# Second layer pair of a gated MLP: three groups of 1024 tokens and two of 768 instead of six of 768

## The chip, the cores and the metric

The program runs on one core of one Trainium2 chip. The metric is the device time of one execution in microseconds, the median of several runs. The profile is of one execution.

## What is computed

A linear-attention layer feeds two feed-forward layers; all inputs and the output are float32. The reference, cut to what matters:

```python
kv = einsum('bhsd,bhse->bhde', k, v)            # 8 batches, 8 heads, 576 tokens, 64 wide
out = einsum('bhsd,bhde->bhse', q, kv)
x = out / sqrt(mean(out * out, -1) + 1e-6) * g_norm     # -> 4608 tokens x 512
x = (sigmoid(x @ w_gate) * (x @ w_val)) @ w_out         # 512 -> 1536 -> 512
h = x @ w_in                                            # 512 -> 2048
g = where(h >= 1, h, where(h <= -1, 0, (h + 1)**2 / 4))
return g @ w_out2                                       # 2048 -> 512
```

## The kernel before

All matrix products run on TensorE with float32 split into two fp32r halves: a product of two tiles is three matmuls (high by high, high by low, low by high). Everything in the program is in an order written out by hand; each engine, and SP's one DMA queue, works through its own instructions in that order, and a wait at the head holds what is behind it.

The first half of the time is attention and the first feed-forward layer, on blocks of 512 tokens. The second layer is the class `Second`, which takes its input from DRAM (`x2d`), where the first layer has stored it.

`Second` works on groups of tokens. A group of 768 tokens is two halves of 384 (T2). For each of eight steps s, two blocks of 128 hidden units for both halves of the tokens are formed by a Strassen-like scheme: seven products instead of eight (`product`, L787), each of two blocks by three matmuls = six matmuls, 128x384. The weights for it (`w_load`, seven sums of blocks, 1792 KB a step) and the sums of input blocks (`x_steps`, tiles x_b11, x_t1 and so on) are made beforehand. The products of a step go to four PSUM banks, A to D, in this order: a11 to A, a12 to D, s1 to B, s2 on top of A, a22 to C, s4 on top of B, s3 on top of A. Between them, ScalarE copies partial sums out (`saved`, tiles p1, p5, u2, u3 in the buffers "sv") and VectorE adds them. The last two readers of A in a step are the copy u3 on ScalarE and VectorE's add into g1, which waits for u3's place in the order. The first bank alternates from step to step: `spare((g + s) % 2)` gives bank A or a bank of the accumulators' pool, "acc2_3".

The activation needs, for each block, a clip and a maximum on VectorE and a square on ScalarE; `finish` (L943) does it for two blocks at once, 768 columns. The results are split into halves (`high` on ScalarE, `low` on VectorE, buffers "gsp", four of them) and are the stationary side of the output products (`out_product`, L813): for each 128 tokens three matmuls 128x512. Two of the four results of a step (first half of the tokens) go into the group's accumulators `acc` while the next step's chain runs: one output product (nine matmuls for three blocks of 128 tokens) stands between s1 and s2 and one behind s3, from step 1 on. The results for the second half of the tokens stay in SBUF (g1) and are multiplied after the eight steps, sixteen output products into `acc2` (banks B, C and the spare one), with the eviction of `acc` (`put`) and the x steps of the next group between them. Only the last group ends its last three output products token by token.

Around the first group: `second.begin()` (L1360) issues `x_load(0)` while the first layer's last pair of blocks still runs. In the last loop of output products there (f = 1 to 11, `down`, twelve matmuls each), each round splits the next g (tiles gh, gl), then runs one x step, then issues weight loads (`stream`, tiles woh), and w_load(0) at f = 4, w_load(1) at f = 9. `second.rest()` then opens the other pools and runs the groups.

In `group`, the order around a step's end is:

```python
self.product(A, "s3", "t3", False)
u3 = self.saved(A, "u3")
tt(g1[s][:, 1], A[:, :T2], s5, ALU.add)
tt(c0[:, 1], C[:, :T2], u3, ALU.add)
if late is not None:
    self.out_product(acc, s - 1 + HF, late_hi, False, False)
```

In step 0 `late` is None and no output product stands there.

Of the kernel before, what the change touches and what calls it, by code (L numbers as in the profile page):

```python
# [17 lines left out]
T2 = 384  # L18
# [15 lines left out]
def attn_gated_mlp_kernel(ctx: ExitStack, tc: tile.TileContext, a: dict, out: bass.AP):  # L34
# [669 lines left out]
    class Second:  # L704
        OPS = ("a11", "a12", "a22", "s1", "s2", "s4", "s3")

        def __init__(self):
            self.stack = ExitStack()
            self.xop = self.pool("xop", 1)
            self.st = self.pool("st", 2)  # L710
            self.tmp = self.pool("tmp2", 1)
            self.half = self.tmp.tile([P, 1], F32, name="half2")
            nc.gpsimd.memset(self.half, 0.5)
            self.ws, self.xo = {}, {}
# [10 lines left out]
        def one(self, name, tag, bufs):  # L725
            return self.tmp.tile([P, T2], F32, name=name, tag=tag, bufs=bufs)

# [3 lines left out]
        def spare(self, n):  # L731

            if n == 0:
                return self.bank("A")
            return self.acc_p.tile([P, T], F32, name="acc2_3", tag="acc2_3")


        def w_load(self, s):
            t = self.st.tile([P, 7, 2, 2 * P], F32R, name="wst", tag="st")
            nc.sync.dma_start(out=t.bitcast(F32), in_=w2d[s])  # L740
            return {name: (t[:, i, 0], t[:, i, 1]) for i, name in enumerate(self.OPS)}


        def x_load(self, g):
            t = self.st.tile([P, 7, 2, 2 * P], F32, name="xin", tag="st")
            t = t.rearrange("p a b n -> p (a b n)")[:, 0:8 * T2].rearrange("p (c n) -> p c n", c=KC)
            step = 2 * P
            for k in range(2):
                for i in range(2 * T2 // step):
                    j, off = divmod(g * 2 * T2 + i * step, T)  # L750
                    c = slice(2 * k, 2 * k + 2)
                    nc.sync.dma_start(out=t[:, c, i * step:(i + 1) * step], in_=x2d[j][:, c, off:off + step])
            return t

        def x_split(self, name, src):
            o = self.xop.tile([P, 2, 2, T2], F32R, name=f"x_{name}", tag=name)
# [4 lines left out]
        def x_steps(self, x):  # L761

            b11, b12, b21, b22 = (x[:, 2 * k:2 * k + 2, e * T2:(e + 1) * T2] for k in range(2) for e in range(2))
            self.x_split("b11", b11)
            yield
            t1 = self.pair("t1")
# [5 lines left out]
            t2 = self.pair("t2")  # L772
# [3 lines left out]
            t4 = self.pair("t4")  # L776
# [5 lines left out]
            t3 = self.pair("t3")  # L782
# [4 lines left out]
        def product(self, bank, w, x, first=True):  # L787
            for c in range(2):
                sl = slice(c * P, (c + 1) * P)
                for n, (h, l) in enumerate(((0, 0), (0, 1), (1, 0))):  # L790
                    nc.tensor.matmul(bank[:, :T2], self.ws[w][h][:, sl], self.xo[x][:, l, c], start=first and c == n == 0,  # L791
                                     stop=c == 1 and n == 2, skip_group_check=True)

        def saved(self, bank, name):
            t = self.one(name, "sv", 4)
            act_copy(t, bank[:, :T2])
# [8 lines left out]
        def high(self, src):  # L805
            o = self.gsp.tile([P, 2, T2], F32R, name="gh2", tag="gsp")
# [6 lines left out]
        def out_product(self, acc, f, g, first, last):  # L813
            w = self.wo2[f]
            for t in range(T2 // P):
                mm3(acc[t], (g[:, 0], g[:, 1]), (w[:, 0], w[:, 1]), first, last, slice(t * P, (t + 1) * P))

        def put(self, acc, t0):
            for t in range(T2 // P):
                e = self.pair("ev2").rearrange("p a b -> p (a b)")[:, :T]  # L820
                (act_copy if t % 2 else dve_copy)(e, acc[t])
                nc.sync.dma_start(out=out[t0 + t * P:t0 + (t + 1) * P, :], in_=e)
# [8 lines left out]
        def rest(self):  # L831
            self.ch_p = self.pool("chain", 1, space=bass.MemoryType.PSUM)
            self.wo2p = self.pool("wo2", 1, "left")
            self.gst = self.pool("gst", 1, "left")
            self.gsp = self.pool("gsp", 4, "left")
            self.acc_p = self.pool("acc2", 1, "left", space=bass.MemoryType.PSUM)
            self.wo2 = {}
            groups = NT // (2 * T2)
            for g in range(groups):
                self.group(g, g + 1 < groups)  # L840
            self.stack.close()

        def group(self, g, more):
            tt, g1 = self.tt, {}
            acc = [self.acc_p.tile([P, T], F32, name=f"acc2_{t}", tag=f"acc2_{t}") for t in range(3)]
            late = None
            for s in range(HF):
                A = self.spare((g + s) % 2)
                D, B, C = (self.bank(n) for n in "DBC")
# [9 lines left out]
                c0 = self.tmp.tile([P, 2, T2], F32, name="c0", tag="c0", bufs=2)  # L859
                g1[s] = self.gst.tile([P, 2, T2], F32, name=f"g1_{s}", tag=f"g1_{s}")  # L860
                self.product(A, "a11", "b11")
                s1 = self.saved(A, "p1")
                if late is not None:
                    vl = self.one("v", "v", 2)
# [4 lines left out]
                tt(c0[:, 0], D[:, :T2], s1, ALU.add)  # L869
# [4 lines left out]
                v = self.one("v", "v", 2)  # L874
# [16 lines left out]
                tt(g1[s][:, 0], B[:, :T2], u2, ALU.add)  # L891
                self.product(A, "s3", "t3", False)
                u3 = self.saved(A, "u3")
                tt(g1[s][:, 1], A[:, :T2], s5, ALU.add)
                tt(c0[:, 1], C[:, :T2], u3, ALU.add)
# [7 lines left out]
            vl = self.one("v", "v", 2)  # L903
# [10 lines left out]
            acc2 = [self.bank("B"), self.bank("C"), self.spare(g % 2)]  # L914
# [3 lines left out]
            kept = []  # L918
# [16 lines left out]
            for t in range(T2 // P if kept else 0):  # L935
                for f, h in kept:
# [505 lines left out]
```

## Time and profile before

| | |
|---|---|
| median of 3 runs | 1711.57 us (1710.27 to 1712.14) |
| the profiled execution | 1714.51 us, its span 1712.7 us |
| TensorE busy | 1699.3 us, 8516 matmuls |
| VectorE, ScalarE busy | 1085.9 us, 815.9 us |
| DMA | 343.45 MB, mean 201 GB/s |
| granted TensorE clock, mean | 0.993 of full speed |
| second layer, first chain product | 961.53 us after the span's start |

Matmuls are pipelined and their ends are modelled, so the time that one takes is read from the distance of two starts, not from its length in a row. Engines are PE (TensorE; PEld its weight loads), DVE (VectorE), ACT (ScalarE), POOL, and SPq (SyncE's DMA queue). L791 is line 791 of the kernel before. In a tile's name the buffer number is left out: chA is a chain bank, acc an accumulator's pool.

### The profile page before, as it was taken

Reading aid. Unit: us, or ns where it says so; the run is one execution under the profiler, and the core shown is the slowest. Engines: PE = TensorE matmul, PEld = TensorE weight load, DVE = VectorE, ACT = ScalarE, POOL = GpSimd, SP = SyncE. Lnnn points to the kernel's source line nnn. Section 1 sums busy time; section 2 is a strip of 40 time slices with the busy share of each in tenths; the row PEclk is TensorE's granted clock in tenths of the full one; section 3 lists DMA queues with packets and bytes.
Section 4 is the critical chain, followed back from the end, with each engine's and each line's share of the span. In section 5 each row is a group of like instructions: output and inputs, shape, how many; then the busy total and the mean of one; then the engine's idle time right before and its main releaser. Section 6 shows DMA issues by size and latency. Waiting matters only on the chain.

```text
span 1712.7 us, 23020 instructions
## 1 busy us (share of the span) xinstructions
PE 1699.3 (99%) x8516; PEld 1437.7 (84%) x8516; DVE 1085.9 (63%) x1909; ACT 815.9 (48%) x1388; POOL 1.0 (0%) x8
## 2 busy tenths in 40 slices
PE   8999999999999999999999999999999999999999
PEld 6778878887877877778887898998998998998997
DVE  5888856767746767775666556556556556556553
ACT  3444444635558667744444444444344344444442
POOL 0000000000000000000000000000000000000000
PEclk8999999999999999999999999999999999999999
DMA  9577877668663987678886764442442542442431
GB/s 263 177 256 239 262 244 234 212 212 266 208 200 122 300 298 239 234 253 307 281 300 211 278 241 150 148 172 99 160 160 99 190 144 90 185 166 104 163 116 37
DMA packets 156832, 343.45 MB, mean 201 GB/s; under 512 B 15400, under 2 KB 64680, under 8 KB 150576
## 3 DMA queue, kind: packets, MB, share of 16 engines
q1 hardware_dynamic: 156720, 341.98, 58.9%
q8 instruction: 67, 1.10, 0.3%
q14 instruction: 45, 0.37, 0.1%
HBM read 264.85 MB, written 77.07 MB: 200 GB/s over the span
## 4 chain that ended last, share of the span: by engine, by line
PE 94%; DMA 2%; DVE 2%; ACT 1%; issue 0%; SPq 0%; ACTq 0%; DVEq 0%
PE acc L96 10%; PE acc L94 10%; PE acc L95 10%; PE h L94 6%; PE chB L791 6%; PE h L96 6%; PE h L95 6%; PE pA L647 6%; PE chA L791 4%; PE acc L791 4%; PE pE L647 4%; PE chC L791 3%; PE chD L791 3%; PE pC L647 2%; PE pD L647 2%; PE chC L96 1%
## 5 line engine op out<-in xcount | busy, mean ns | idle before, releaser
L94 PE MATMUL acc<-gh,woh 128*128 128x512 f32 x420 | 165.7, 395 | 2.1 <-DMA woh<-wo1d 2.1
L95 PE MATMUL acc<-gl,woh 128*128 128x512 f32 x420 | 164.4, 391 | 0.3 <-DVE gl L77 0.3
L94 PE MATMUL h<-xh,w 128*128 128x512 f32 x384 | 151.8, 395 | 1.2 <-DVE xn L302 1.2
L96 PE MATMUL h<-xh,w 128*128 128x512 f32 x384 | 150.0, 391 | 0.0
L95 PE MATMUL h<-xl,w 128*128 128x512 f32 x384 | 149.8, 390 | 0.0
L96 PE MATMUL acc<-wo,gh 128*128 128x512 f32 x336 | 132.4, 394 | 0.0
L95 PE MATMUL acc<-wo,gh 128*128 128x512 f32 x336 | 132.2, 394 | 0.0
L94 PE MATMUL acc<-wo,gh 128*128 128x512 f32 x336 | 130.9, 390 | 0.0
L96 PE MATMUL acc<-gh,woh 128*128 128x512 f32 x324 | 126.6, 391 | 0.0
L647 PE MATMUL pA<-xc,wc 128*128 128x512 f32 x432 | 110.2, 390 | 0.5 <-ACT s L69 0.5
L69 ACT ACTIVATE gh<-g 128x384 fp32r<-128x384 f32 (+1 forms) x120 | 63.6, 541 | 73.5 <-PE acc L96 51.7
L94 PEld LDWEIGHTS acc<-gh,woh 128*128 128x128 f32 x420 | 78.9, 188 | 22.3 <-ACT gh L69 3.2
L647 PEld LDWEIGHTS pA<-xc,wc 128*128 128x128 f32 x432 | 80.9, 188 | 18.1 <-ACT s L69 1.2
L95 PEld LDWEIGHTS acc<-gl,woh 128*128 128x128 f32 x420 | 78.9, 188 | 17.8 <-DVE gl L77 1.3
L94 PEld LDWEIGHTS h<-xh,w 128*128 128x128 f32 x384 | 72.2, 188 | 23.2 <-issue 5.9
L720 DVE TENSOR_TENSOR gh<-c,gh 128x384 fp32r<-128x384 f32 x96 | 53.6, 558 | 57.6 <-ACT gh L69 56.9
L720 DVE TENSOR_TENSOR c<-chD,p 128x384 f32<-128x384 f32 x48 | 26.8, 558 | 92.1 <-ACT v L803 81.4
L96 PEld LDWEIGHTS h<-xh,w 128*128 128x128 f32 x384 | 72.2, 188 | 15.2
L95 PEld LDWEIGHTS h<-xl,w 128*128 128x128 f32 x384 | 72.2, 188 | 14.3
L569 DVE TENSOR_TENSOR gf<-sig,h 128x512 f32<-128x512 f32 x57 | 39.1, 686 | 71.1 <-PE h L96 40.4
L720 DVE TENSOR_TENSOR g<-vp,g 128x768 f32<-128x768 f32 x48 | 46.0, 959 | 48.3 <-ACT vp L803 48.3
L96 PEld LDWEIGHTS acc<-wo,gh 128*128 128x128 f32 x336 | 63.0, 188 | 13.6
(236 smaller groups left out, 3828.7 us busy)
## 6 DMA issues: line engine op xcount, KB each, us to landing
wst<-w2d SPq DMA_DIRECT2D x48, 1792.0 KB, 7.4
wc<-w1d SPq DMA_DIRECT2D x168, 256.0 KB, 5.3
woh<-wo1d SPq DMA_DIRECT2D x162, 256.0 KB, 5.0
raw<-in_w SPq DMA_DIRECT2D x32, 512.0 KB, 6.0
raw<-in_w_gv SPq DMA_DIRECT2D x24, 512.0 KB, 5.1
w1d<-w2half SPq DMA_DIRECT2D x48, 256.0 KB, 3.3
w2d<-w2half SPq DMA_DIRECT2D x48, 256.0 KB, 3.9
kvraw<-in_kv_main SPq DMA_DIRECT2D x24, 448.0 KB, 5.6
```

Of the source, the lines that this page charges most:

```text
L69: nc.scalar.activation(out=o, in_=i, func=AF.Copy)
L94: nc.tensor.matmul(ps, w[0][:, wsl], x[0], start=first, stop=False)
L95: nc.tensor.matmul(ps, w[0][:, wsl], x[1], start=False, stop=False)
L96: nc.tensor.matmul(ps, w[1][:, wsl], x[0], start=False, stop=last)
L569: nc.vector.tensor_tensor(out=g, in0=sig, in1=value, op=ALU.mult)
L647: nc.tensor.matmul(o, w[:, h, sl], x[c][l], start=first and c == n == 0, stop=c == 1 and n == 2, skip_group_check=True)
L720: nc.vector.tensor_tensor(out=o, in0=x, in1=y, op=op)
L791: nc.tensor.matmul(bank[:, :T2], self.ws[w][h][:, sl], self.xo[x][:, l, c], start=first and c == n == 0, stop=c == 1 and n == 2, skip_grou ...
```

## The change

Groups are of 2 x 512, 2 x 512, 2 x 512, 2 x 384 and 2 x 384 tokens. A wide group has four blocks of 128 tokens in each half and so four accumulators; the banks are now A, D, B, C for the chain and acc2_0 to acc2_3, and the first product of every step uses A. All tiles have room for 512 columns and are cut to the group's width. To fit, there are two "pair" buffers instead of three, three "sv" and three "gsp" instead of four; `finish` takes its two blocks one after the other through the "v" buffers, and `put` uses "sv" and "v" buffers. `put` handles one block of 128 tokens; for `acc` it is called after output products 1 to 4, one block each. The last three output products of every group are done token block by token block, each block's eviction right behind. `x_load` moves pieces of up to 512 columns instead of 256. The scratch pool and its constant are opened in `rest`, on the other side of SBUF.

```diff
-T2 = 384
+SIZES = (512, 512, 512, 384, 384)
 ...
-    def pair(self, name):
-        return self.tmp.tile([P, 2, T2], F32, name=name, tag="pair", bufs=3)
+    def pair(self, name, n):
+        return self.sums.tile([P, 2, T], F32, name=name, tag="pair")[:, :, :n]
 ...
     def x_load(self, g):
-        step = 2 * P
+        n = 2 * SIZES[g]
+        t = self.st.tile([P, KC, 2 * T], F32, name="xin", tag="st")[:, :, :n]
+        begin = 2 * sum(SIZES[:g])
         for k in range(2):
+            c, at = slice(2 * k, 2 * k + 2), 0
+            while at < n:
+                j, off = divmod(begin + at, T)
+                step = min(T - off, n - at)
+                nc.sync.dma_start(out=t[:, c, at:at + step], in_=x2d[j][:, c, off:off + step])
+                at += step
 ...
-    def put(self, acc, t0):
-        for t in range(T2 // P):
-            e = self.pair("ev2").rearrange("p a b -> p (a b)")[:, :T]
+    def put(self, acc, t0, t):
+        e = self.one("ev2", *(("sv", 3), ("v", 2))[t == 3], T)
 ...
     def group(self, g, more):
-        acc = [self.acc_p.tile([P, T], F32, name=f"acc2_{t}", tag=f"acc2_{t}") for t in range(3)]
+        n2 = self.n = SIZES[g]
+        tokens = range(n2 // P)
+        acc = [self.acc_p.tile([P, T], F32, name=f"acc2_{t}", tag=f"acc2_{t}") for t in tokens]
         for s in range(HF):
-            A = self.spare((g + s) % 2)
-            D, B, C = (self.bank(n) for n in "DBC")
+            A, D, B, C = (self.bank(n) for n in "ADBC")
 ...
-        acc2 = [self.bank("B"), self.bank("C"), self.spare(g % 2)]
+        acc2 = [self.bank(n) for n in "ADBC"[-len(tokens):]]
         for n, f in enumerate(order):
-            if not more and n >= F2 - 3:
-                kept.append((f, ready.pop(n)))
-            else:
-                self.out_product(acc2, f, ready.pop(n), n == 0, n == F2 - 1)
+            if n < F2 - 3:
+                self.out_product(acc2, f, ready.pop(n), n == 0, False)
             if n == 1:
                 self.finish(g1[HF - 1])
                 self.out_product(acc, F2 - 1, late_hi, False, True)
-                self.put(acc, g * 2 * T2)
+            if 0 < n <= len(tokens):
+                self.put(acc, t0, n - 1)
 ...
-        self.put(acc2, g * 2 * T2 + T2)
+        for t in tokens:
+            for n in range(F2 - 3, F2):
+                self.out_product(acc2, order[n], ready[n], False, n == F2 - 1, (t,))
+            self.put(acc2, t0 + n2, t)
 
     def finish(self, c):
-        v = self.pair("vp")
-        self.clip(v, c)
-        self.square(v)
-        self.tt(c, v, c, ALU.max)
+        for e in range(2):
+            v = self.one("v", "v", 2, self.n)
+            self.clip(v, c[:, e])
+            self.square(v)
+            self.tt(c[:, e], v, c[:, e], ALU.max)
```

## Rows read from the trace of the kernel before

**Rows 1.** The page: busy time of each engine, then the chain's shares.

```profile
PE 1699.3 (99%) x8516; PEld 1437.7 (84%) x8516; DVE 1085.9 (63%) x1909; ACT 815.9 (48%) x1388; POOL 1.0 (0%) x8
...
PE 94%; DMA 2%; DVE 2%; ACT 1%; issue 0%; SPq 0%; ACTq 0%; DVEq 0%
```

**Rows 2.** Windows, first group: stretch, length, busy time by engine, clock, DMA, GB/s.

```profile
961.53:1086.07 124.54, 124.54 (x625) 112.70 (x624) 70.24 (x127) 53.56 (x98) 0.00 (x0) 1.00 0.57 213
```

**Rows 3.** Timeline, TensorE in one step: start, length, engine, line, operation, idle before.

```profile
1244.02 0.39 PE L94 MATMUL acc<-wo,gh 128*128 128x512 f32 x1
...
1246.10 1.23 PE L791 MATMUL acc<-x_t,wst 128*128 128x384 f32 x6
1247.17 1.20 PE L791 MATMUL chC<-x_t,wst 128*128 128x384 f32 x6
1248.21 1.20 PE L791 MATMUL chB<-x_b,wst 128*128 128x384 f32 x6
```

**Rows 4.** Timeline, TensorE in the first layer's pair loop, one step apart.

```profile
728.33 1.52 PE L647 MATMUL pC<-xc,wc 128*128 128x512 f32 x6
...
740.57 1.52 PE L647 MATMUL pC<-xc,wc 128*128 128x512 f32 x6
```

**Rows 5.** Timeline and page: around step ends, A's readers, finish; an add at 512.

```profile
1217.88 1.20 PE L791 MATMUL acc<-x_b,wst 128*128 128x384 f32 x6
...
1218.08 0.49 ACT L69 ACTIVATE u<-chA 128x384 f32<-128x384 f32 x1 [1.63 <-PE chA L791]
1218.61 0.56 DVE L720 TENSOR_TENSOR g<-chA,p 128x384 f32<-128x384 f32 x1 [0.94 <-ACT u L69]
...
1247.35 0.55 DVE L800 TENSOR_SCALAR vp<-g 128x768 f32<-128x768 f32 x1
...
1247.93 0.94 ACT L803 ACTIVATE vp<-vp,half 128x768 f32<-128x768 f32 x1
...
1251.08 0.56 DVE L720 TENSOR_TENSOR g<-acc,p 128x384 f32<-128x384 f32 x1 [0.75 <-ACT u L69]
...
1252.38 1.23 PE L791 MATMUL chA<-x_b,wst 128*128 128x384 f32 x6
...
L569 DVE TENSOR_TENSOR gf<-sig,h 128x512 f32<-128x512 f32 x57 | 39.1, 686 | 71.1 <-PE h L96 40.4
```

**Rows 6.** Timeline, first layer: a product that waits for the copy of its bank.

```profile
585.34 0.58 ACT L69 ACTIVATE s<-pA 128x512 f32<-128x512 f32 x1
...
585.98 1.66 PE L647 MATMUL pA<-xc,wc 128*128 128x512 f32 x6 [0.53 <-ACT s L69]
```

**Rows 7.** Timeline, the last output products of the first layer: splits and x steps.

```profile
949.31 0.68 DVE L77 TENSOR_TENSOR gl<-g,gh 128x512 fp32r<-128x512 f32 x1
...
950.89 0.85 ACT L69 ACTIVATE x_t<-t 128x768 fp32r<-128x768 f32 x1 [1.97 <-DVE t L720]
...
951.77 0.96 DVE L720 TENSOR_TENSOR x_t<-t,x_t 128x768 fp32r<-128x768 f32 x1 [0.91 <-ACT x_t L69]
...
952.65 0.68 DVE L77 TENSOR_TENSOR gl<-g,gh 128x512 fp32r<-128x512 f32 x1
...
953.42 0.47 PE L95 MATMUL acc<-gl,wok 128*128 128x512 f32 x1
```

**Rows 8.** Timeline: SP's issue of weight loads, and TensorE's wait for them.

```profile
931.53 7.35 SPq L540 DMA_DIRECT2D woh<-wo1d  x12
...
936.61 0.47 PE L94 MATMUL acc<-gh,woh 128*128 128x512 f32 x1 [1.06 <-DMA woh<-wo1d]
```

**Rows 9.** DMA issues, 1075 to 1100 us: count, size, median us to landing.

```profile
wst<-w2d SPq DMA_DIRECT2D x2, 1792.0 KB, 7.3
out<-ev SPq DMA_DIRECT2D x3, 256.0 KB, 2.5
```

**Rows 10.** Windows, as rows 2: near the start, and around a wait.

```profile
25.00:30.00 5.00, 4.73 (x40) 3.66 (x44) 2.53 (x5) 1.36 (x4) 0.00 (x0) 0.50 1.08 258
...
935.00:940.00 5.00, 3.94 (x17) 2.78 (x16) 1.65 (x2) 1.57 (x3) 0.00 (x0) 1.00 1.02 367
```

More of the change, by code (lines that the diff above doesn't have):

```diff
@@ L761, in x_steps @@
         def x_steps(self, x):
-            b11, b12, b21, b22 = (x[:, 2 * k:2 * k + 2, e * T2:(e + 1) * T2] for k in range(2) for e in range(2))
+            n = x.shape[-1] // 2
+            b11, b12, b21, b22 = (x[:, 2 * k:2 * k + 2, e * n:(e + 1) * n] for k in range(2) for e in range(2))
             self.x_split("b11", b11)
             yield
-            t1 = self.pair("t1")
+            t1 = self.pair("t1", n)
             self.tt(t1, b12, b11, ALU.subtract)
@@ L771, in x_steps @@
             yield
-            t2 = self.pair("t2")
+            t2 = self.pair("t2", n)
             self.tt(t2, b22, t1, ALU.subtract)
@@ L775, in x_steps @@
             yield
-            t4 = self.pair("t4")
+            t4 = self.pair("t4", n)
             self.tt(t4, b21, t2, ALU.subtract)
@@ L781, in x_steps @@
             yield
-            t3 = self.pair("t3")
+            t3 = self.pair("t3", n)
             self.tt(t3, b22, b12, ALU.subtract)
@@ L790, in product @@
                 for n, (h, l) in enumerate(((0, 0), (0, 1), (1, 0))):
-                    nc.tensor.matmul(bank[:, :T2], self.ws[w][h][:, sl], self.xo[x][:, l, c], start=first and c == n == 0,
+                    nc.tensor.matmul(bank[:, :self.n], self.ws[w][h][:, sl], self.xo[x][:, l, c], start=first and c == n == 0,
                                      stop=c == 1 and n == 2, skip_group_check=True)
         def saved(self, bank, name):
-            t = self.one(name, "sv", 4)
-            act_copy(t, bank[:, :T2])
+            t = self.one(name, "sv", 3, self.n)
+            act_copy(t, bank[:, :self.n])
             return t
@@ L811, in low, with out_product @@
             self.tt(o[:, 1], src, o[:, 0].bitcast(F32), ALU.subtract)
[L813 removed]
+        def out_product(self, acc, f, g, first, last, tokens=None):
             w = self.wo2[f]
[L815 removed]
+            for t in range(len(acc)) if tokens is None else tokens:
                 mm3(acc[t], (g[:, 0], g[:, 1]), (w[:, 0], w[:, 1]), first, last, slice(t * P, (t + 1) * P))
[L818 to L822 removed]
+        def put(self, acc, t0, t):
+            e = self.one("ev2", *(("sv", 3), ("v", 2))[t == 3], T)
+            (act_copy if t % 2 else dve_copy)(e, acc[t])
+            nc.sync.dma_start(out=out[t0 + t * P:t0 + (t + 1) * P, :], in_=e)
         def wo2_load(self, f):
@@ L833, in rest @@
             self.wo2p = self.pool("wo2", 1, "left")
+            self.tmp = self.pool("tmp2", 1, "left")
+            self.gsp = self.pool("gsp", 3, "left")
             self.gst = self.pool("gst", 1, "left")
-            self.gsp = self.pool("gsp", 4, "left")
             self.acc_p = self.pool("acc2", 1, "left", space=bass.MemoryType.PSUM)
+            self.half = self.tmp.tile([P, 1], F32, name="half2")
+            nc.gpsimd.memset(self.half, 0.5)
             self.wo2 = {}
-            groups = NT // (2 * T2)
-            for g in range(groups):
-                self.group(g, g + 1 < groups)
+            for g in range(len(SIZES)):
+                self.group(g, g + 1 < len(SIZES))
             self.stack.close()
@@ L902, in group @@
             ready = {}
-            vl = self.one("v", "v", 2)
+            vl = self.one("v", "v", 2, n2)
             self.clip(vl, late)
```

47 lines of the change are left out of this document (16 added, 31 removed).

## The prediction, made before the change was run

> **What bounds the kernel now.** I read the page's busy times first, then the chain of waits, then the second layer's stretch by group, then its timeline. TensorE is busy 99% of the span and holds 94% of the chain that ended last [rows 1]. In the second layer it never stops: a group of 768 tokens takes 124.54 us and PE is busy for all of it, at full clock, with VectorE at 70 us and ScalarE at 54 us [rows 2]. All six groups look like that; the middle ones take 124.53 us. So here a change is worth what it takes from TensorE's own stream, minus every wait that it puts in front of TensorE; work saved on the other engines or on DMA is worth nothing by itself.
>
> The timeline gives the price of the stream. Two chain products of six 128x384 matmuls start 1.04 us apart (1247.17 to 1248.21), so one costs 173 ns. The nine output matmuls ahead of a product last 2.08 us (1244.02 to 1246.10), and the product behind them 1.07 us instead of 1.04 [rows 3]. In the first layer pair the same seven products and one output product of twelve, all 512 wide, repeat every 12.24 us (728.33 to 740.57): 54 matmuls at 226.7 ns, changes between the two kinds included [rows 4]. Nine at that pitch would be 2.04 us, so in the second layer each change-over costs 0.04 + 0.03 = 0.07 us that the 512-wide loop does not pay.
>
> **The change, part by part.** *Wider products.* Before, there are 6 x 8 x 7 = 336 products of 1.04 us = 349.4 us. After, 168 products of six 512-wide matmuls at 1.36 us (6 x 226.7 ns) and 112 of 1.04 us: 345.0 us. That is -4.5 us: the same columns, 336 matmuls fewer. The output products stay 1728 in number of matmuls. The change-overs occur 14 times a group (two a step, none in a group's first step): 84 before, 28 in the two groups of 768 after, so 56 x 0.07 = -3.9 us, -4.0 from the unrounded starts. A 1024 group then needs 720 x 226.7 ns = 163.2 us, and 3 x 163.2 + 2 x 124.53 = 738.7 against 747.2: **-8.5 us**. If the change-overs stay, it is -4.5.
>
> The fixed part of a matmul decides this term. Here 173.3 and 226.7 ns differ by 53.3 ns for 128 columns at the granted 2.4 GHz, which leaves 13.3 ns for each matmul whatever its width [rows 3, 4]. The Trainium skill (TensorE: Matmul & The Clock Gate, "Back-to-back issue gap") puts it at about 2.5 ns over N/2.4. By that an estimate of the chain's gain is 336 x 2.5 ns = 0.8 us instead of 4.5, and the sum below would end 3.7 us later. The trace disagrees for these fp32r pairs of weight load and matmul, and the measured pitch decides.
>
> *One bank for the first chain.* Today the first product of a step alternates between two banks, so step 1's a11 starts at 1217.88, without a wait, although the bank of the product that just ended is read by ScalarE from 1218.08 and by VectorE until 1218.61 + 0.56 = 1219.17 [rows 5]. After, both use bank A, and TensorE, which works in order, has to wait for these two readers. From step 1 on, an output product stands between: A is free at 1251.08 + 0.56 = 1251.64 and wanted at 1252.38, 0.74 us later [rows 5]; with 512 the output product is 12 matmuls = 2.72 us against readers of 1.5 us, so about 1.1 us are left. `finish` in two halves stands on VectorE ahead of these readers. It starts within 0.2 us of s2's end (1247.17, clip at 1247.35 [rows 3, 5]); until the copy of A ends there are three products, 0.20 and the copy, 4.9 us at 512, of which the add on B takes 0.6. Two halves of clip 0.45, square 0.75 (estimates, from 0.55 and 0.94 at 768), maximum 0.69 and 0.12 of hops take 4.0 us [rows 5], so they end 0.3 us early and cost nothing. In step 0 there is no output product in between, so each group pays once. At 384: 0.20 to the copy's start, copy 0.49, 0.04, add 0.56, and the wake of TensorE. A wait of that kind is in the trace: a copy ends at 585.92, the product starts at 585.98 and takes 1.66 us instead of 1.52 [rows 4, 6], so 0.06 + 0.14. Sum 1.49 us. At 512 the copy takes 0.58 [rows 6] and an add 0.69 [rows 5]: 1.71 us. Behind the waiting product stand only TensorE's own instructions; ScalarE and VectorE have just done what they had. 3 x 1.71 + 2 x 1.49 = **+8.1 us**. Bounds: 6.5 (five times 1.29, no wake, 384 lengths) to 9 (another 0.2 us at each).
>
> *Wider tiles for group 0, beside the first layer's last output products.* The x steps run on ScalarE and VectorE between the splits (gh, gl) that TensorE needs every 2.72 us. In a step with a subtraction the loop is gl, t, x_t on ScalarE, x_t's low half, next gl: 949.31 to 952.65 = 3.34 us, longer than 2.72, and by the second of two such steps gl ends at 953.33 and TensorE resumes 0.08 us late [rows 7]. The slack is used up exactly there. With 1024 columns the two VectorE operations grow by 0.27 each (0.56 at 384, 0.96 at 768) and the copy by 0.24 (0.49 and 0.85) [rows 5, 7]: 0.78 a step. Two steps in a row: 1.56 us of wait, and some 0.2 at the last one, t3. **+1.75 us**, bounds 0 and 2.5.
>
> *x_load for 1024 tokens* goes in four DMAs of 512 KB instead of six of 256 KB, through SP's one queue, ahead of the `woh` loads that TensorE already waits 1.06 us for [rows 8]. Twelve of those, 3 MB, are issued in 7.35 us [rows 8], so 0.5 MB more is +1.2 us at most; if the longer rows move faster, the 1.06 us go. I take 0, the middle, and keep -1.06 and +1.2.
>
> *The rest at nothing.* Weight loads fall from 48 to 40, under a TensorE that doesn't wait for them. Three `gsp` buffers let the high half start when product n starts, 5.4 us (4.1 at 384) before it is needed, against 1.7 of work. All groups now end their last three output products token by token, so all but the last eviction lie under matmuls and bank A is free before the next group; the kernel's end has the same order as today. `put` borrows the chain's `sv` buffers (third rival). Scratch moved to the left side opens over first-layer tiles that are read by then, or whose stores have landed before the slots are written.
>
> **Sum:** -8.5 + 8.1 + 1.75 + 0 = +1.35 us. It is made on the profiled execution, whose span is 1712.7 us with 1.8 us around it (1714.51, 2.9 above the runs' median); nothing outside the span changes, so I carry the difference to the median: 1711.57 + 1.35 = 1712.9 us. Its own range: -3.1 (the wait at 6.5, the `woh` wait gone) to +5.4 (the change-overs stay).
>
> **Rivals.**
> *Bank A late in every step (slower).* If finish's two halves hold VectorE past the 1.1 us of room, not only step 0 waits but the six that follow in each of the three wide groups: 18 times. It decides from that point; each 0.1 us beyond it is 1.8 us, and 0.3 us gives 1712.9 + 5.4 = 1718.3. For it: twice the hops between the two engines, and only 0.3 us to spare ahead of the room. Against it: the rows' lengths leave room.
>
> *The gain without its price (faster).* The change may not cost TensorE the wait, if bank A's readers are done or the order lets other work in between: -8.5 + 1.75, 1704.8 us. For it: the gain is plain in two pitches. Against it: in step 0 nothing stands behind s3 but a11, and its readers end 1.29 us later [rows 5].
>
> *The borrowed buffers (slower).* p1 of a new group takes the buffer of the first eviction, whose store is queued behind 1792 KB of weights. A store alone lands in 2.5 us, the weights in 7.3 [rows 9]. If p1 must wait for both, s2 on the same bank is late at the four boundaries by up to 1 us each, at most 1.5 at the narrow one: +3, 1715.9 us. Against it: with three token blocks of 2.04 us between the eviction and p1, there is about as much time as that.
>
> *The clock falls in the new waits (slower).* At the start, with TensorE in pieces, a stretch of 5 us ran at 0.50, the 1.2 GHz level; around a wait of 1.06 us later on it stayed at 1.00 [rows 8, 10]. If each of the five longer waits brought one such stretch, half of 5 us is lost each time: +12.5, 1725.4 us. The Trainium skill (TensorE: Matmul & The Clock Gate, "A second HAM failure mode: psum-queue depth-cycling") describes such a loss where matmul groups pause in turning over PSUM banks; the trace shows none so far for a pause of 1.06 us, and no row shows one of 1.7.
>
> **How the numbers follow.** Forecast 0.66, bank A late in every step 0.09, gain without price 0.15, buffers 0.07, clock 0.03. About 0.2% (3.4 us) is what a measurement of this kernel can tell from no change. Of the forecast's 0.66, 0.08 lies above +3.4 and the rest within; of the gain without price 0.02 falls within. Faster 0.13, within 0.2% 0.60, slower 0.08 + 0.09 + 0.07 + 0.03 = 0.27. The range goes from the forecast's low end, 1711.57 - 3.1, some 1708.4, to the first rival's 1718.3: outside stay most of the gain without price, the clock and a worse first rival, just under 2 in 10.
>
> **What would show it.** Right: products of 1.36 us as in rows 4 and no slow product behind the output block in the first three groups; one PE wait of about 1.6 us at the second step of each group, released by VectorE's add on chA, five in all and none elsewhere; groups of about 165 and 126 us; the last output products of the first layer 1.5 to 2 us longer with waits for gl; clock 1.00 throughout. Wrong: groups of 163 us (the price is not paid), waits for A in later steps, ScalarE's p1 waiting for a store at a group's start, or a `woh` wait of over 2 us.

## The result, and the profile after

The changed kernel takes 1732.88 us (median of 4 runs, 1731.97 to 1737.31) against 1710.92 (4 runs, 1710.18 to 1712.14): ratio 1.0125, 95% interval 1.0106 to 1.0145. It is slower by 1.25%, six times what a measurement can tell, and outside the forecast range. The profiled execution takes 1732.97 us, its span is 1730.9.

First the windows of the five groups, then of one short stretch (columns as in [rows 2]):

```profile
964.02:1131.72 167.70, 166.23 (x722) 135.11 (x721) 90.49 (x144) 67.71 (x107) 0.00 (x0) 1.00 0.44 162
1299.50:1467.41 167.91, 166.50 (x722) 135.02 (x720) 87.46 (x143) 66.33 (x107) 0.00 (x0) 1.00 0.31 110
1467.41:1595.66 128.25, 126.32 (x625) 112.64 (x624) 71.50 (x142) 55.56 (x106) 0.00 (x0) 1.00 0.38 138
1595.66:1730.90 135.24, 128.05 (x625) 114.10 (x623) 63.32 (x133) 49.71 (x98) 0.00 (x0) 0.99 0.29 105
1602.10:1605.50 3.40, 3.40 (x13) 3.40 (x12) 1.14 (x3) 1.52 (x3) 0.00 (x0) 0.50 0.00 0
```

Groups of about 165 and 126 us were forecast; they take 167.7 and 128.3. TensorE is again busy for all but 1.5 us of a wide group, so most of the excess is not a wait: the same work runs slower. The timeline of TensorE shows where. One step, and then two first matmuls of output products behind the chain, twelve matmuls apart:

```profile
1062.02 1.52 PE L787 MATMUL chA<-x_t,wst 128*128 128x512 f32 x6
1063.38 0.39 PE L94 MATMUL acc<-wo,gh 128*128 128x512 f32 x1
...
1066.17 1.54 PE L787 MATMUL chA<-x_b,wst 128*128 128x512 f32 x6
1067.55 1.53 PE L787 MATMUL chD<-x_b,wst 128*128 128x512 f32 x6
1068.92 1.29 PE L787 MATMUL chB<-x_t,wst 128*128 128x512 f32 x5
...
1092.52 0.40 PE L94 MATMUL chA<-wo,gh 128*128 128x512 f32 x1
...
1095.32 0.40 PE L94 MATMUL chA<-wo,gh 128*128 128x512 f32 x1
```

A chain product takes 1.36 us (1062.02 to 1063.38), as forecast. The twelve output matmuls beside it take 2.79 (1063.38 to 1066.17), 232.3 ns each, and the product behind them 1.38 (to 1067.55). Behind the chain twelve take 2.80 us (1092.52 to 1095.32): 233.3 ns. There the kernel before took 2.04 us for nine, 226.7 ns:

```profile
1051.39 0.39 PE L94 MATMUL chB<-wo,gh 128*128 128x512 f32 x1
...
1053.43 0.39 PE L94 MATMUL chB<-wo,gh 128*128 128x512 f32 x1
```

So the slow pace has reached all 1728 output matmuls, not only those at a change-over.

Then the waits of TensorE in the second layer (waited for: us in total, times, longest):

```profile
PE chA L787 <- DVE g L718: 6.6, 5, 1.5
PE chA L787 <- ACT p L69: 3.0, 2, 2.2
```

The five of the first row are the forecast wait for bank A, and no later step waits for A's readers. The two waits for p1 were not in the sum; they are the prediction's third rival. The longer one, in the timeline:

```profile
1591.61 0.33 SPq L733 DMA_DIRECT2D wst<-w2d  x1
...
1594.04 2.87 SPq L817 DMA_DIRECT2D out<-ev  x3
...
1600.65 0.49 ACT L69 ACTIVATE p<-chA 128x384 f32<-128x384 f32 x1 [6.29 <-DMA out<-ev]
...
1601.19 1.53 PE L787 MATMUL chA<-x_t,wst 128*128 128x384 f32 x6 [2.21 <-ACT p L69]
...
1602.52 2.12 PE L787 MATMUL chC<-x_t,wst 128*128 128x384 f32 x6
...
1604.44 1.70 PE L787 MATMUL chB<-x_b,wst 128*128 128x384 f32 x6
```

The weights of the next step are issued at 1591.61, the stores of the evictions behind them, and p1 can't be written before the store that reads its buffer has landed, 6.29 us after ScalarE is ready. TensorE waits 2.21 us, and then its clock is at 0.50, the 1.2 GHz level, for 3.4 us (last window above): chC takes 1.92 us instead of 1.04.

Last, the end of the first layer, beside which the x tiles are made:

```profile
930.92 8.62 SPq L540 DMA_DIRECT2D woh<-wo1d  x12
...
936.70 0.47 PE L94 MATMUL acc<-gh,woh 128*128 128x512 f32 x1 [2.06 <-DMA woh<-wo1d]
...
937.85 0.50 PE L96 MATMUL acc<-gh,woh 128*128 128x512 f32 x1 [0.44 <-DMA woh<-wo1d]
...
955.53 0.50 PE L95 MATMUL acc<-gl,wok 128*128 128x512 f32 x1 [0.85 <-DVE gl L77]
```

The waits for `woh` are 2.06 and 0.44 us where [rows 8] had 1.06, and gl is late by 0.85 us where the prediction read 0.08 from [rows 7].

Summed by starts of matmuls: from the first layer's last chain product to the second layer's first it took 38.08 us before and 41.47 after (+3.39); from there to the last matmul 746.94 and 762.68 (+15.74). What lies ahead was 0.91 us shorter, so the spans differ by 18.2. The start of the second layer scatters between 956 and 967 us over all profiles here, whatever the kernel, so in what follows versions are compared by the length of the second layer, and by medians of their runs where the whole counts.

### The profile page after: what moved, and what is told of

It is laid out like the page before. It is cut to its first block, busy times and chain, and to the rows that moved or that the text cites. A ratio compares the mean times of both kernels' runs of the same rounds, so it can differ in the third digit from the quotient of the medians.

```text
span 1730.9 us, 22267 instructions
## 1 busy us (share of the span) xinstructions
PE 1705.0 (99%) x8180; PEld 1391.8 (80%) x8180; DVE 1076.8 (62%) x1862; ACT 809.9 (47%) x1337; POOL 1.0 (0%) x8
## 3 DMA queue, kind: packets, MB, share of 16 engines
q8 instruction: 65, 1.06, 0.3%
## 4 chain that ended last, share of the span: by engine, by line
PE 91%; DVE 3%; DMA 3%; ACT 2%; issue 1%; SPq 0%; ACTq 0%; DVEq 0%
PE chA L787 9%; PE acc L94 9%; PE acc L96 9%; PE acc L95 9%; PE h L94 6%; PE h L95 6%; PE h L96 6%; PE chB L787 6%; PE pA L647 6%; PE pE L647 4%; PE chC L787 3%; PE chD L787 3%; PE pD L647 2%; PE pC L647 2%; PE kvps L159 2%; DMA woh<-wo1d 1%
## 5 line engine op out<-in xcount | busy, mean ns | idle before, releaser
L799 ACT ACTIVATE v<-v,half 128x512 f32<-128x512 f32 (+1 forms) x160 | 107.8, 674 | 58.3 <-DVE v L796 58.3
L787 PE MATMUL chA<-x_t,wst 128*128 128x512 f32 (+1 forms) x480 | 113.2, 371 | 3.0 <-ACT p L69 3.0
L96 PE MATMUL acc<-wo,gh 128*128 128x512 f32 x288 | 114.2, 396 | 0.0
L94 PE MATMUL acc<-wo,gh 128*128 128x512 f32 x288 | 113.5, 394 | 0.0
L95 PE MATMUL acc<-wo,gh 128*128 128x512 f32 x288 | 113.2, 393 | 0.0
L69 ACT ACTIVATE gh<-g 128x512 fp32r<-128x512 f32 (+1 forms) x104 | 61.8, 594 | 107.8 <-PE chC L96 81.4
L787 PEld LDWEIGHTS chA<-x_t,wst 128*128 128x128 f32 x480 | 88.0, 188 | 17.3 <-ACT p L69 4.2
L718 DVE TENSOR_TENSOR c<-chD,p 128x512 f32<-128x512 f32 (+1 forms) x40 | 25.5, 638 | 119.4 <-PE chD L787 71.0
L718 DVE TENSOR_TENSOR g<-v,g 128x512 f32<-128x512 f32 (+1 forms) x80 | 51.1, 638 | 74.4 <-ACT v L799 74.4
L647 PEld LDWEIGHTS pA<-xc,wc 128*128 128x128 f32 x432 | 80.8, 188 | 18.2 <-ACT s L69 1.2
L95 PEld LDWEIGHTS acc<-gl,woh 128*128 128x128 f32 x420 | 78.9, 188 | 18.2 <-DVE gl L77 1.6
L718 DVE TENSOR_TENSOR gh<-g,gh 128x512 fp32r<-128x512 f32 (+1 forms) x80 | 50.8, 636 | 66.5 <-ACT gh L69 66.5
```

What stands on the lines that cost most here:

```text
L69: nc.scalar.activation(out=o, in_=i, func=AF.Copy)
L94: nc.tensor.matmul(ps, w[0][:, wsl], x[0], start=first, stop=False)
L95: nc.tensor.matmul(ps, w[0][:, wsl], x[1], start=False, stop=False)
L96: nc.tensor.matmul(ps, w[1][:, wsl], x[0], start=False, stop=last)
L647: nc.tensor.matmul(o, w[:, h, sl], x[c][l], start=first and c == n == 0, stop=c == 1 and n == 2, skip_group_check=True)
L718: nc.vector.tensor_tensor(out=o, in0=x, in1=y, op=op)
```

## The experiments

For every run: start addresses modulo 256 bytes of wo2 (columns that stream in an output product), gh2 (its weights) and the chain's operands (x tiles and wst, which agree), as the program places them; the median and its ratio to the kernel before on the same chip; the length of the second layer; and the distance of two matmuls in ns: output matmuls beside the chain and behind it, and in the chain product right behind an output block, 384 or 512 wide (means over 156 to 1025 matmuls). "Beside the chain" are the 756 output matmuls that stand in blocks of nine or twelve between chain products, "behind" the 972 after a group's eight steps. The medians of the kernel before that were taken along with these versions lie between 1710.9 and 1714.3 us, so two rows that were not measured together compare through the ratio.

| version | wo2, gh2, chain | us | ratio (95%) | layer 2 | out, beside / behind | 384 / 512 |
|---|---|---|---|---|---|---|
| before | 128, 128, 224 | 1710.9 | | 746.9 | 231.6 / 226.9 | 178.1 / - |
| b_gsp32 | 128, 160, 224 | 1718.5 | 1.0022 to 1.0050 | 754.1 | 232.1 / 233.3 | 178.5 / - |
| b_all0 | 128, 128, 192 | 1706.2 | 0.9955 to 0.9981 | 742.0 | 228.0 / 226.7 | 173.6 / - |
| b_256 | 128, 128, 128 | 1710.3 | 0.9983 to 1.0004 | 746.5 | 231.2 / 226.9 | 177.7 / - |
| after | 128, 160, 224 | 1732.9 | 1.0106 to 1.0145 | 762.7 | 232.3 / 233.3 | 178.5 / 230.3 |
| a_gsp0 | 128, 192, 224 | 1734.7 | 1.0103 to 1.0143 | 763.7 | 233.0 / 233.3 | 178.1 / 231.5 |
| a_all0 | 128, 192, 192 | 1730.8 | 1.0091 to 1.0121 | 761.7 | 233.0 / 233.3 | 173.6 / 230.0 |
| a_256 | 128, 128, 128 | 1720.4 | 1.0032 to 1.0070 | 752.0 | 228.2 / 226.9 | 177.6 / 226.7 |
| a_256_ev | same | 1716.7 | 1.0017 to 1.0043 | 746.8 | 228.2 / 226.8 | 177.7 / 226.7 |
| a_256_evA | same | 1707.9 | 0.9969 to 0.9989 | 738.4 | 228.2 / 226.9 | 177.7 / 226.6 |
| a_narrow1 | same | 1702.9 | 0.9924 to 0.9959 | 738.4 | 228.2 / 226.9 | 177.7 / 226.7 |
| a_narrow1_32 | 128, 128, 192 | 1704.8 | 0.9934 to 0.9968 | 739.2 | 227.7 / 226.9 | 173.6 / 230.3 |
| a_narrow1_first | as a_256 | 1705.4 | 0.9935 to 0.9968 | 738.4 | 228.2 / 226.9 | 177.7 / 226.7 |
| a_narrow1_shift | 128, 128, 128 or 192 | 1700.7 | 0.9914 to 0.9952 | 736.9 | 227.1 / 226.8 | 173.6 / 226.7 |

**Why are the output matmuls slow?** In the kernel before, the scratch pool lay on the right side of SBUF and gh2 at 91264 in a partition. After, the pool lies on the left ahead of gh2, and its first tile, one constant, moves everything behind it by 32 bytes; also, the low half now lies 2048 bytes behind the high one. Two edits to each kernel tell these apart.

a_gsp0:
```diff
-self.half = self.tmp.tile([P, 1], F32, name="half2")
+self.half = self.tmp.tile([P, 16], F32, name="half2")[:, 0:1]
```


> The kernel after, with one constant's tile widened from 4 to 64 bytes, so that the tiles gh2 (stationary side of all output products) start at multiples of 64 bytes as in the kernel before; in the kernel after they start 32 bytes off. Everything else as after (1732.9 us). Theory address: it is this offset that holds the output matmuls at 233.3 ns; then the 972 behind the chain run at 226.7 ns as before and the time falls by 972 x 6.6 ns = 6.4 us, to 1726.5; the 756 beside the chain stay at 232, as they were before. Rival geometry (the low half lies 2048 bytes behind the high one instead of 1536, or twelve matmuls a block instead of nine, or four accumulators): no change, 1732.9 and 233.3 ns.

a_all0 and b_all0 (the first with the edit above too):
```diff
+self.pool("pad", 1).tile([P, 1], F32, name="pad")
 self.xop = self.pool("xop", 1)
```


> As the run before, and an unused tile of 32 bytes is put ahead of the chain's weights and x tiles, so that they too start at multiples of 64 bytes; before and after they start 32 bytes off. Theory address, in its wider form (a change of offset between two matmuls is what costs): the 756 output matmuls beside the chain also run at 226.7 ns, and the chain product behind each block too: another 756 x 5.6 ns = 4.2 us and 42 + 28 products x some 0.02 us = 1.4 us, to about 1721. In its narrow form (the offset of gh2 alone): 1726.5, as the run before. Rival geometry: 1732.9.

> The kernel before with the unused tile of 32 bytes ahead of the chain's weights and x tiles, so that all operands of the second layer's matmuls start at multiples of 64 bytes. Theory address, wider form: the change-overs stop costing, 84 x 0.07 = 5.9 us, to about 1705. Narrow form and rival: no change, 1710.9.

b_gsp32:
```diff
+self.pool("pad", 1, "left").tile([P, 1], F32, name="pad")
 self.gst = self.pool("gst", 1, "left")
```


> The kernel before with an unused tile of 32 bytes ahead of g1 and gh2, so that they start 32 bytes off as in the kernel after. Theory address: the output matmuls behind the chain, 1728 - 756 = 972, rise from 226.7 to 233.3 ns: +6.4 us, to 1717.3. Rival geometry: no change, 1710.9.

Two first matmuls of blocks behind the chain, nine matmuls apart in b_gsp32 and twelve apart in a_gsp0 (timelines):

```profile
1052.68 0.40 PE L94 MATMUL chB<-wo,gh 128*128 128x512 f32 x1
...
1054.78 0.40 PE L94 MATMUL chB<-wo,gh 128*128 128x512 f32 x1
```

```profile
1090.80 0.40 PE L94 MATMUL acc<-wo,gh 128*128 128x512 f32 x1
...
1093.60 0.40 PE L94 MATMUL chA<-wo,gh 128*128 128x512 f32 x1
```

In b_gsp32 nine take 2.10 us, 233.3 ns: 32 bytes of unused tile, with no other edit, give the kernel before the slow pace of the kernel after and 7.1 us in the second layer (6.4 expected). So the place does it, and geometry isn't needed. But a_gsp0's expectation failed: at a multiple of 64 bytes twelve still take 2.80 us. a_all0's failed too: 1730.8 where the wider form had about 1721; only the 384-wide product behind a block became fast (173.6 ns). That looked like the rival. b_all0 spoke against it: 32 bytes ahead of the chain alone took 4.9 us from the kernel before, most of it at the change-overs, which the wider form had put at 5.9. Nine output matmuls beside its chain, first start to the chain product behind them:

```profile
1243.44 0.39 PE L94 MATMUL acc<-wo,gh 128*128 128x512 f32 x1
...
1245.49 0.68 PE L792 MATMUL chA<-x_b,wst 128*128 128x384 f32 x3
```

They take 2.05 us where [rows 3] have 2.08. So the places of the two operands matter, but not modulo 64. I put each 512-wide matmul of the six profiles beside the distance of two addresses, that of the next matmul's weights and that of the columns streaming meanwhile: modulo 256 bytes, at a distance of 0 nearly nine in ten kept 226.7 ns, at 32, 64 or 128 nine in ten or more didn't. Most of the exceptions at 0 stand beside the chain or right behind an output block. The next four runs test that, and then the other costs one at a time.

b_256 and a_256 (a_256 also with the constant's tile at 64 elements):
```diff
+self.pool("pad", 1).tile([P, 24], F32, name="pad")
 self.xop = self.pool("xop", 1)
```


> The kernel before with 96 bytes of unused tile ahead of the chain's tiles, so that wst, the x tiles, gh2 and wo2 all start at the same place modulo 256 bytes (128). Theory phase: a matmul is followed at 226.7 ns (512 columns) where the weights of the next one and the columns that stream in this one start at the same place modulo 256 bytes, at some 233 otherwise (so it stands in the rows of the six kernels run so far, 97 in 100 and 9 in 10). Then the 756 matmuls beside the chain fall from 231.6 to 226.7 and the chain product behind each block from 177.8 to 173.3 ns a matmul: 3.7 + 504 x 4.5 ns = 2.3, 6 us below before, 0.9 below the version with 32 bytes (ratio 0.9965). Rival, 64 bytes: only the place modulo 64 counts, then it is as with 32 bytes (0.997, 228.0 ns).

> The kernel after, all operands of the second layer's matmuls at the same place modulo 256 bytes: the constant's tile widened to 256 bytes, 96 bytes of unused tile ahead of the chain's tiles. Theory phase: all 1728 output matmuls run at 226.7 ns instead of 232.3 and 233.3 (756 x 5.6 + 972 x 6.6 ns = 10.6 us) and the product behind each block loses its 0.02 to 0.03 us (70 x 0.025 = 1.8): 12.4 us below after, 1720.5, some 1.005 of before. Rival geometry (low half 2048 bytes behind the high one, blocks of twelve, four accumulators): no change, 1732.9, 233.3 ns.

The block of twelve in a_256 again, and TensorE's waits there:

```profile
1085.46 0.39 PE L94 MATMUL chA<-wo,gh 128*128 128x512 f32 x1
...
1088.18 0.39 PE L94 MATMUL chA<-wo,gh 128*128 128x512 f32 x1
```

```profile
PE chA L788 <- DVE g L719: 6.6, 5, 1.5
PE chA L788 <- ACT p L69: 4.2, 3, 2.4
```

Twelve take 2.72 us: 226.7 ns with halves 2048 bytes apart, blocks of twelve and four accumulators. The geometry is cleared, and 12.5 us are back (1732.9 to 1720.4, with 12.4 expected). That these two agree so closely is partly luck: the second layer lost 10.7, not 12.4. By the table's means the pace makes some 10.2 of it (756 x 4.1 + 972 x 6.4 + 252 x 3.6 ns); the stretch at half clock, which of these two profiles only that of after has, makes 1.7, and 1.2 more in waits for p1 goes the other way. The change-overs in the wide groups cost nothing any more: beside the 512-wide chain the output matmuls run at 226.7 ns, and so does the product behind a block. In the narrow groups they still cost (231.2 and 177.6 ns; the table's 228.2 is the mean of both), and b_256 missed for the same reason. One change-over of b_256:

```profile
1241.65 0.39 PE L94 MATMUL acc<-wo,gh 128*128 128x512 f32 x1
...
1243.73 1.23 PE L792 MATMUL acc<-x_t,wst 128*128 128x384 f32 x6
1244.80 1.20 PE L792 MATMUL chC<-x_t,wst 128*128 128x384 f32 x6
```

Its 2.08 and 1.07 us are those of [rows 3]: with a chain 384 wide, distance 0 keeps the old price, and the 64 bytes of b_all0 had suited it. So the rule is not "equal places are fast" for every pair of widths.

a_256_ev:
```diff
 def put(self, acc, t0, t, end=False):
+    if end:
+        if t % 2 == 0:
+            self.ev = self.pair("ev2", T)
+        e = self.ev[:, t % 2]
+    else:
+        e = self.one("ev2", *(("sv", 3), ("v", 2))[t == 3], T)
...
-self.put(acc2, t0 + n2, t)
+self.put(acc2, t0 + n2, t, True)
```


> As the run before, and the evictions of the second accumulators at a group's end go to the two buffers of the x sums (two halves each) instead of the chain's sv and v buffers; so no p1 stands behind a store. Theory buffers: the waits of TensorE for p1 at the two boundaries to a narrow group (1.099 - 0.227 = 0.87 us and 2.548 - 0.227 = 2.3 us) go, and with the second the stretch of 3.4 us at a granted clock of 0.5 (1.7 us): 4.9 us below the run before, 1715.6. Rival: the chain's next wait (c on VectorE, the weights) is as late, then under 1 us is gained.

a_256_evA:
```diff
-A, D, B, C = (self.bank(n) for n in "ADBC")
+D, B, C = (self.bank(n) for n in "DBC")
+if s:
+    A = self.bank("A")
+elif len(acc) == 4:
+    A = acc[3]
+else:
+    A = self.acc_p.tile([P, T], F32, name="acc2_3", tag="acc2_3")
```


> As the run before, and the first step of each group uses a bank of the accumulators' pool (acc2_3, idle then) in place of A, as the kernel before did by turns; so a11 of the second step finds A free. Theory bank: the five gaps of 1.63, 1.57, 1.57, 1.28 and 1.28 us (over the pitch) go: 7.3 us below the run before, 1708.3, under before. Rival: TensorE then waits at the next thing in the second step (g1's sums, the split for the first output product), and less than 3 us come back.

Windows of a wide and a narrow group in a_256_ev, then in a_256_evA; the last two are of the first layer's end in a_256_evA:

```profile
965.49:1130.54 165.05, 163.58 (x722) 135.13 (x720) 90.48 (x144) 67.71 (x107) 0.00 (x0) 1.00 0.45 165
1460.54:1586.53 125.99, 124.76 (x626) 112.65 (x625) 71.46 (x142) 55.59 (x106) 0.00 (x0) 1.00 0.39 140
```

```profile
966.81:1130.06 163.25, 163.25 (x721) 135.22 (x720) 90.49 (x144) 67.83 (x107) 0.00 (x0) 1.00 0.45 167
1456.57:1581.02 124.45, 124.45 (x625) 112.68 (x624) 71.54 (x142) 55.70 (x106) 0.00 (x0) 1.00 0.39 142
...
935.00:940.00 5.00, 2.80 (x7) 2.01 (x8) 1.92 (x2) 0.99 (x2) 0.00 (x0) 0.69 0.98 354
940.00:945.00 5.00, 5.00 (x15) 3.93 (x15) 1.76 (x3) 1.58 (x2) 0.00 (x0) 0.62 1.06 415
```

With the buffers apart the second layer loses 5.2 us, and the groups are the forecast's own: 165.05 and 125.99. The 4.9 that was expected was right by luck: 1.7 of it was a stretch at half clock, which the profile of a_256 doesn't have behind its longest wait (2.39 us, up to 1587.83),

```profile
1585.00:1590.00 5.00, 2.61 (x15) 2.29 (x14) 1.47 (x3) 1.60 (x3) 0.00 (x0) 1.00 0.42 163
```

and a_256 had a third wait for p1, of 0.92 us, at a boundary between two wide groups. With a free bank the second layer loses 8.3 more (7.3 expected), TensorE is busy for the whole of every group, and the version passes the kernel before. In its first layer the waits for `woh` (1.9 and 0.9 us) are followed by a granted clock of 0.69 and 0.62 in two windows of 5 us: 44.55 us from the last chain product to the second layer. That is the place of the next edit.

a_narrow1:
```diff
-SIZES = (512, 512, 512, 384, 384)
+SIZES = (384, 512, 512, 512, 384)
```


> As the last version (all operands at one place modulo 256 bytes, evictions in the x sums' buffers, a free bank for the first step), with the groups in the order 768, 1024, 1024, 1024, 768 tokens; so the x tiles made beside the first layer's last output products are 384 wide again and their load 1.5 MB instead of 2. Theory x tiles and load: from the first layer's last chain matmul to the second layer's first one it took 38.1 us in the kernel before and 41.1 to 44.6 in the versions of after; it returns to some 38, 3.3 us less (and up to 6 where TensorE fell to half clock behind its two waits there): 1704.6. The second layer stays at 738.4 us. Rival: the load of the weights that TensorE waits for is late for another reason than the wider x load; then some 1.6 us come back, 1706.3.

TensorE's waits at the first layer's end in a_narrow1:

```profile
PE acc L94 <- DMA woh<-wo1d: 1.1, 1, 1.1
PE acc L95 <- DVE gl L77: 0.3, 1, 0.3
```

They are those of the kernel before, and the stretch is 38.10 us again. With a wide first group it took 41.0 to 44.6 us in all six profiles, with a narrow one 37.8 to 38.5 in seven of eight (the eighth is a_narrow1_first, below), so the wider first group was the cause; what the load and what the tiles had in it was not tested apart. The whole gains 5.0 us on a_256_evA's median (3.3 expected, up to 6 with the clock); by the ratios, which allow for the kernel before's own medians of 1711.3 and 1714.3, it is some 6.5.

a_narrow1_32 is a_narrow1 with a tile of 8 elements in place of 24 in front of the chain. (In the next two expectations "the run before" and "the first of these three" are a_narrow1.)

> As the run before with 32 bytes of unused tile ahead of the chain's tiles instead of 96, so the chain stands 64 bytes off the output products modulo 256, as in the version of before that ran 84 change-overs without their price (228.0 and 173.6 ns). Theory phase in its simple form (equal places are fast, others slow): the output matmuls beside the chain in the wide groups rise from 226.7 to 228 or more and the product behind them too, 42 x 0.05 = 2 us more; nothing is gained in the narrow groups. Rival, the offset of 64 suits a change-over: the 28 change-overs of the narrow groups lose 0.066 us each, 1.8 us less, and the wide ones stay.

A 512-wide product right behind an output block, and the next one, in a_narrow1_32:

```profile
1109.10 1.54 PE L788 MATMUL chA<-x_b,wst 128*128 128x512 f32 x6
1110.49 1.54 PE L788 MATMUL chD<-x_b,wst 128*128 128x512 f32 x6
```

Both theories had a part: at 64 the 512-wide product behind a block is slow (1.39 us), the 384-wide one fast (173.6 ns). Together the second layer is 0.8 us longer.

a_narrow1_first:
```diff
 m, r, t = (tp.tile([P, TC, H], F32, name=f"early_{n}", tag=f"e{n}") for n in "mrt")
+tp.tile([P, 32], F32, name="pad1", tag="pad1")
```


> As the first of these three, and an unused tile of 128 bytes in the first layer's scratch, ahead of the buffers woh and wok that stand 128 bytes off g modulo 256. Theory phase: the 288 output matmuls between 188 and 265 us and the last twelve before the second layer, at 233.3 ns in all kernels so far, run at 226.7: 300 x 6.6 ns = 2.0 us less than the first of these three. Rival: the first layer's slow stretch comes from VectorE's and ScalarE's splits of the same weights; no change.

First matmuls of blocks in the first layer, nine matmuls apart, in the kernel after and then in this version:

```profile
235.43 0.39 PE L94 MATMUL acc<-gh,woh 128*128 128x512 f32 x1
...
237.53 0.39 PE L94 MATMUL acc<-gh,woh 128*128 128x512 f32 x1
```

```profile
236.06 0.39 PE L94 MATMUL acc<-gh,woh 128*128 128x512 f32 x1
...
238.09 0.39 PE L94 MATMUL acc<-gh,woh 128*128 128x512 f32 x1
```

2.10 us become 2.03, and the mean over the stretch from 188 to 265 us falls from 233.4 to 227.4 ns, in a loop that the change didn't touch. So the cost follows the place there too. The whole didn't get faster (1705.4 against 1702.9, intervals overlapping), so the forecast 2.0 us are not shown in the time: the first output product of the first layer starts anywhere between 183 and 190 us over the profiles. In this profile TensorE also waits 1.6 and 0.8 us at the first layer's end, with a granted clock of 0.76 in the 5 us behind (41.1 us instead of 38.1). So that stretch can be long with a narrow first group too; why it was here stays open.

a_narrow1_shift:
```diff
-o = self.xop.tile([P, 2, 2, T], F32R, name=f"x_{name}", tag=name)[:, :, :, :src.shape[-1]]
+o = self.xop.tile([P, 2, 2, T], F32R, name=f"x_{name}", tag=name)
+at = 0 if src.shape[-1] == T else 16
+o = o[:, :, :, at:at + src.shape[-1]]
...
-t = t.rearrange("p c n -> p (c n)")[:, 0:28 * P].rearrange("p (a b n) -> p a b n", a=7, b=2)
+at = 0 if SIZES[g] == T else 16
+t = t.rearrange("p c n -> p (c n)")[:, at:at + 28 * P].rearrange("p (a b n) -> p a b n", a=7, b=2)
```


> As the version with the narrow group first, and in the narrow groups alone the chain's weights and x tiles start 64 bytes further on (a slice of their tiles), so the chain stands 64 bytes off the output products there and at the same place in the wide groups. Theory, taken from the rows of the runs so far (a 384-wide chain beside 512-wide output products is fast at 64, a 512-wide chain at 0): the 28 change-overs of the narrow groups lose nine times 4.5 and six times 4.3 ns each, 1.8 us; the second layer takes 736.6 us instead of 738.4, all output matmuls run at 226.7 to 228, and the time is some 1701 (ratio 0.993). Rival: what counts is one place for all, then the narrow groups gain nothing, or the step from 64 to 0 between groups brings the slow pace into the wide ones, 2 us more.

```profile
960.33:1084.06 123.73, 123.73 (x626) 112.35 (x624) 74.19 (x143) 57.26 (x106) 0.00 (x0) 1.00 0.58 212
1084.06:1247.31 163.25, 163.25 (x721) 135.13 (x720) 91.02 (x144) 67.25 (x106) 0.00 (x0) 1.00 0.33 119
```

The narrow group takes 123.73 us instead of 124.45, the wide one stays at 163.25, the second layer 736.9 (736.6 expected). 1700.74 us, ratio 0.9933 (0.9914 to 0.9952): ahead of both kernels, with the shortest second layer of all versions. That the whole is faster than a_narrow1 (0.9924 to 0.9959) is not shown.

## Why the prediction was wrong

Its sum was -8.5 + 8.1 + 1.75 + 0. Taken apart by the runs, on one profile of each, it was -8.5 + 8.3 + 3.4 + 10.7 + 5.2 = 19.1, of which an earlier start took back 0.9: wider products and change-overs, the bank, the end of the first layer, the place of the tiles, the buffers of `put`.

*Wider products, -4.5: right.* 1.36 and 1.04 us in every version. The measured pitch with 13.3 ns fixed per matmul held. The Trainium skill (TensorE: Matmul & The Clock Gate, "Back-to-back issue gap") gives 2.5 ns for an isolated matmul, not for a stream; by it an estimate of this term is 0.8 us. The second layer's -8.5 in a_256_evA, -4.5 and -4.0, does not agree with that.

*Change-overs vanish, -4.0: the step that failed.* I read 0.07 us in the narrow loop and none in the 512-wide loop of the first layer [rows 3, 4] and took the width for the cause. The place of the tiles was part of it: in the first layer's loop all operands lie at one place modulo 256 bytes, in the second layer they didn't, and after the change they did so less. The size of 4.0 was right: a_256_evA, wide groups at one place, ends at -8.5, 746.94 to 738.44, where 738.7 stood in the forecast. But the kernel after kept the price (232.3 ns beside the chain, 230.3 in the 512-wide product behind a block) and took the slow pace into the 972 output matmuls that had been free of it: 10.7 us between after and a_256, some 10.2 of it the pace. The prediction put this side of the edit at nothing, in one sentence, that scratch "opens over first-layer tiles that are read by then"; no rival named it, and no row of before showed a moved tile. The slow pace itself was to be seen, unexplained, at 188 to 265 us of the trace of before.

*One bank, +8.1: right.* Five waits, none elsewhere; taking them away gave 8.3. The first of them, in the timeline of after:

```profile
973.80 0.60 ACT L69 ACTIVATE u<-chA 128x512 f32<-128x512 f32 x1 [2.41 <-PE chA L787]
974.43 0.69 DVE L718 TENSOR_TENSOR g<-chA,p 128x512 f32<-128x512 f32 x1 [1.30 <-ACT u L69]
...
975.18 1.66 PE L787 MATMUL chA<-x_b,wst 128*128 128x512 f32 x6 [1.47 <-DVE g L718]
```

Copy, add and start come in the forecast order; from the last start of s3 to that of a11 it is 1.86 us instead of 0.23, 1.63 more, where 1.71 was forecast.

*x tiles, +1.75, and the load, 0 with bounds -1.06 and +1.2: the load mis-sized.* Together they are 3.4: the `woh` waits grew by 1.4 us, outside the bound, and what is left for the x tiles is 2.0, inside theirs; the waits for gl that the profiles name are only 0.9 of it (1.2 against 0.3). a_narrow1 gives all of it back. That the longer rows of the load might make up for its half MB more did not come true. The low end of the whole range, -3.1, was also said with too few terms: the wait at 6.5 and the `woh` wait gone give -8.5 + 6.5 + 1.75 - 1.06 = -1.3; -3.1 needs the x tiles at 0 as well.

*The rest at nothing: failed for `put`.* That was the third rival, priced at 3 and given 0.07. It came at both boundaries to a narrow group, where less time lay between eviction and p1 than the weights and a store took, and in a_256 once between wide groups. Its cost differs from profile to profile: in after it is two waits, 3.0 us, and 1.7 of half clock; in a_256 three waits, 4.2, without the clock, and there taking it away gave 5.2. Finish in two halves, three gsp buffers and the end cost nothing that a_256_evA shows.

*Rivals.* Bank A late in every step: it didn't happen. Gain without price: not in this kernel. The clock: once in the second layer, behind a wait for p1 and not behind a wait for bank A. The third rival came true in part; the largest cost, the place of the tiles, was none of the four, and a range drawn only from them could not hold it.

## What to carry to other kernels

Before a change that moves tiles is priced by its instructions, note where its matmul operands will start: here an unused tile of 32 bytes cost the kernel before 7.1 us of its second layer in one spot and saved 4.9 in another, beside the 8.5 that the wider groups bring. The place alone did not decide the sign: a_256 was still slower than the kernel before (1.0051), and only with the buffers and the bank set right as well did the change gain. A pace that differs between two loops is to be explained before it is carried from one to the other. And a buffer shared with a store was as late here as what was queued ahead of that store.

## What the runs showed that I had not expected

The distance of two fp32r matmuls of 512 columns is near one of two values here, 226.7 and 233.3 ns, at a granted clock of 1.00, and start addresses set which. Behind the chain it is the fast one where weights and streaming columns start at one place modulo 256 bytes (distance 0: a_256), the slow one at 32 (b_gsp32, after) and 64 (a_gsp0); in the first layer's output products it is fast at 0 and slow at 128 (a_narrow1_first against after). Where output products alternate with a chain, the chain's place counts too: with 384 columns 64 bytes off was fast and 0 and 96 were not (b_all0, b_256, before); with 512 columns the product right behind a block was fast at 0 and not at 64 (226.7 in a_256, 230.3 in a_narrow1_32). What in the chip does it, no run shows, and neither that 256 is the whole period.

The clock doesn't follow from a wait's length alone: after 2.21 us it was at 0.50 for 3.4 us, after 2.39 us at the same place in a_256 it stayed at 1.00, and after two waits of 1.9 and 0.9 us close together (a_256_evA) two windows of 5 us had a mean of 0.69 and 0.62.
